# Two raw weight tiles fetched and decoded later, and v loaded in groups of 1, 1, 2 and 8 pairs, in an attention and MoE kernel

## The chip, the cores and the metric

The kernel runs on one core of one Trainium2 chip. The metric is the device time of one execution in microseconds; the time of a kernel is the median of its runs.

## The reference

Causal attention, then two small dense networks, all in fp32. There are 2 batches of 12 heads, 448 positions and a head size of 64, so 896 tokens of width 768. Cut to what is computed:

```python
scores = np.where(mask, -1e9, q @ k.T / sqrt(64))     # per batch and head, causal
attn = softmax(scores) @ v                            # 1e-9 is added to the sum
x = heads side by side                                # 896 x 768
h = max(max(x @ w1, x @ w2), x @ w3) @ w_out          # first network, 768 wide
g = s * relu(h @ w_in)**2 + b                         # second network, 2048 wide
return g @ moe2_w_out
```

## The kernel before, in words

**Precision.** Each fp32 operand of a large product is held as a high and a low part, and three products (high by high, high by low, low by high) are summed in PSUM. The weights arrive raw, as 56 tiles of 128x768 64-bit words (768 KB each), and every raw tile is decoded on the chip into its high and low part (`decoder`, lines 132 to 190). The steps of one decode are: `high` (line 144, ACT) and `low` (line 147, ACT), which read the raw tile; `clamp` (line 153, DVE); `shift` (line 166, DVE); `sign` (line 172, DVE, which reads the raw tile a last time); `add` (line 179, DVE); `hi` (line 184, ACT); `lo` (line 92, DVE).

**Attention.** The 12 batch-and-head pairs (two heads each) go through a software pipeline of steps, `step(s)` for s = 0 to 13 (line 551). In step s pair s has its scores computed on TensorE (lines 350 to 388), its row minima taken on DVE (line 396) and its exponentials on ACT (line 408). Pair s-1 is transposed (line 435) and copied out of PSUM (line 441, pieces 0 to 2 by ACT, piece 3 by DVE); its row sums are transposed (`sums`, line 480), copied on DVE to `rows` (line 487), written to a small DRAM buffer `rcd` by two DMAs (`spread`, lines 488 and 489) and read back spread over the partitions into `rb` by two DMAs (`broadcast`, line 497). Pair s-2 is multiplied by v (`pv`, lines 451 to 460) into the one PSUM bank `o`. Pair s-3 is scaled by its `rb` out of `o` (`pv_out`, line 506, DVE, tile `xf`, then POOL lines 296 and 92). So `pv` of a pair waits until `xf` of the pair before has emptied `o`, and `xf` waits until that pair's `rb` has landed.

**Engine order.** Every engine runs its instructions in the order in which the program gives them; nothing is reordered. ACT has one decode operation at the end of a step at most, behind all exponentials of that step and ahead of those of the next one (`END`, line 34); DVE has its own in the middle (`MID`, line 29) or at the end. Where a decode step stands is written out by hand in these two tables.

**The DMA queue.** All loads leave through SP's queue (except one store). Its order in a step is: the two `rcd` writes (their `rows` must be there), the q and k of pair s+4 (`load`, line 268, tile `R`, 448 KB), the first count of v loads, the broadcast of pair s-1 (the `rcd` writes must have landed), the second count of v loads, and a raw weight tile (`fetch_w`, line 125, the DMA of line 129) if the step stands in `FETCH` (line 27). v is loaded in 42 DMAs of line 289: the pairs are cut into groups (`V_GROUPS`, line 39: first pair and number of pairs), each group has one SBUF tile and comes as 7 row pieces, once for a group of one pair, once for each of the two heads otherwise, so 7, 7, 14 and 14 DMAs. `V_LOADS` (line 40) has the two counts of each step. In the kernel before, raw tiles are asked for in steps 0 (no pair is there to broadcast, so `fetch_w` is called in its place), 1, 4, 8, 10 and 11.

**After attention** the products of the two networks run on TensorE (lines 698 and 807) with the decoded weights; the decode goes on beside them, and the first two decoded tiles are used already in steps 12 and 13, to fill TensorE.

Line 551 and the tables above it are what the change touches. The functions are below.

Of the kernel before, what the change touches and what calls it, by code (L numbers as in the profile page):

```python
# [23 lines left out]
TQ = 128  # L24
NQ = 3

FETCH = (1, 4, 8, 10, 11)
LAST = 9
MID = {
    2: ("clamp0",), 3: ("shift0",), 4: ("sign0",), 5: ("add0",), 6: ("lo0",), 7: ("clamp1",),  # L30
    8: ("shift1",), 9: ("sign1",), 10: ("add1",), 11: ("lo1",), 12: ("add2", "clamp3"),
    13: ("lo2", "shift3"),
}
END = {
    1: ("high0",), 2: ("low0",), 3: ("high1",), 4: ("low1",), 5: ("hi0",), 6: ("high2",),
    7: ("low2",), 8: ("clamp2",), 9: ("shift2",), 10: ("hi1", "sign2"), 11: ("high3",),
    12: ("hi2", "low3"),
}
V_GROUPS = ((0, 1), (1, 1), (2, 4), (6, 6))
V_LOADS = ((7, 7), (2, 5), (3, 4), (3, 0), (3, 0), (3, 0), (3, 0), (2, 0))  # L40
FILL = {12: (3, 5), 13: (0, 4)}
WARM = 10
BUSY = (7,)
# [7 lines left out]
def kernel(  # L51
# [73 lines left out]
    def fetch_w():  # L125
        if w_src:
            src = w_src.pop(0)
            raw = wr_p.tile([128, DM], I64, tag="wraw", name="wraw")
            nc.sync.dma_start(out=raw, in_=src)
            raws.append(raw)  # L130
# [101 lines left out]
    def attention():  # L232
        with ExitStack() as c2:
# [10 lines left out]
            vs = [  # L244
                fixed.tile([128, n, 2, NQ + 1, D], F32, name=f"v{a}") for a, n in V_GROUPS
            ]
# [26 lines left out]
            def v_loads(g):  # L273
                (first, n), V = V_GROUPS[g], vs[g]
                for a, b in pieces:
                    rows, src = slice(a % 128, a % 128 + b - a), slice(a % CH, a % CH + b - a)
                    to, of = V[rows, :, :, a // 128], v[first:first + n, src, :, a // CH]
                    if n == 1:
                        yield to[:, 0], of[0]
                    else:  # L280
                        for h in range(2):
                            yield to[:, :, h], of[:, :, h].rearrange("p k d -> k p d")

            v_list = [e for g in range(len(V_GROUPS)) for e in v_loads(g)]

            def load_v(n):
                for _ in range(min(n, len(v_list))):
                    to, of = v_list.pop(0)
                    nc.sync.dma_start(out=to, in_=of)  # L289

            def v_of(p):
                g = max(g for g, (a, _) in enumerate(V_GROUPS) if a <= p)
                return vs[g][:, p - V_GROUPS[g][0]]

# [197 lines left out]
            def broadcast(p):  # L492
                e = pair[p]
                flat = e["flat"]
                for h in range(2):
                    at = h * (NQ + 1) * 128
                    nc.sync.dma_start(
                        out=e["rb"][hs[h]], in_=flat[:, at:at + S].to_broadcast([D, S])
                    )
# [51 lines left out]
            def step(s):  # L551
                new, old, out, nxt = (
                    p if 0 <= p < n_pairs else None for p in (s, s - 1, s - 2, s + 2)
                )
                loads = V_LOADS[s] if s < len(V_LOADS) else (0, 0)
                if new is not None:
# [95 lines left out]
                if old is not None:  # L652
                    load_v(loads[0])
                    broadcast(old)
                else:
                    fetch_w()
                load_v(loads[1])
                if s in FETCH:
                    fetch_w()
                if s == LAST:  # L660
                    nc.sync.dma_start(out=sb[:, 0:1], in_=s2.to_broadcast([128, 1]))
                    nc.sync.dma_start(out=sb[:, 1:2], in_=b2.to_broadcast([128, 1]))
# [19 lines left out]
            for s in range(n_pairs + 2):  # L682
                step(s)
# [196 lines left out]
```

## Time and profile before

| what | us |
|---|---|
| median of 3 runs | 503.01 (501.52 to 503.52) |
| the profiled execution's own time | 502.06 |
| its span in the profile | 500.3 |
| TensorE busy (matmul) | 493.3, 99% of the span |
| DVE, ACT, POOL busy | 340.5, 282.9, 71.4 |

The span is from the first to the last instruction that the profiler saw; the time of an execution has 1.8 us more around it. TensorE's granted clock is at its upper level in all 40 slices of the page. Attention takes about the first 93 us of the span; then come the products of the networks, in which TensorE is the whole chain.

### The profile page before, as it was taken

The page shows a single profiled execution, that of the slowest core. Times are in us where ns is not written, and L with a number is a line of the kernel's source. Part 1 is how long each engine was busy: PE and PEld are TensorE (multiplying, and loading weights), DVE is VectorE, ACT ScalarE, POOL GpSimd, SP SyncE. Part 2 cuts the span into 40 slices and gives each one's busy share as a digit, 9 for nine tenths or more (in the row PEclk, how much of TensorE's full clock was granted, in tenths as well). Part 3 has the DMA queues.
Part 4 walks back from the last instruction along what each step waited for, and adds up shares of the span by engine and source line. Part 5 has one row for each costly group of instructions (what it writes and reads, how often), then busy time and mean ns, then how long its engine had stood idle before and what let it go on. Part 6 is the DMA issues. An engine that isn't in the chain of part 4 may idle for free.

```text
span 500.3 us, 7557 instructions
## 1 busy us (share of the span) xinstructions
PE 493.3 (99%) x2909; PEld 452.7 (90%) x2909; DVE 340.5 (68%) x512; ACT 282.9 (57%) x527; POOL 71.4 (14%) x103
## 2 busy tenths in 40 slices
PE   8999999999999999999999999999999999999997
PEld 4877888899999999999999999999999999999996
DVE  5778896665857667587677888888888644484401
ACT  5988977444445254444546878888786432253101
POOL 6988992300000000000000000000000000000000
PEclk9999999999999999999999999999999999999999
DMA  5777534223324231333223323332333323261003
GB/s 170 225 215 226 151 102 117 103 91 127 126 75 148 94 126 64 126 128 126 101 89 126 127 73 118 126 104 85 127 126 109 119 89 128 88 220 56 1 0 111
DMA packets 26212, 58.34 MB, mean 117 GB/s; under 512 B 13548, under 2 KB 17600, under 8 KB 26176
## 3 DMA queue, kind: packets, MB, share of 16 engines
q1 hardware_dynamic: 26032, 57.76, 35.2%
q8 instruction: 23, 0.38, 0.3%
q14 instruction: 13, 0.11, 0.1%
q10 hardware_dynamic: 144, 0.10, 0.1%
HBM read 55.05 MB, written 2.80 MB: 116 GB/s over the span
## 4 chain that ended last, share of the span: by engine, by line
PE 91%; DMA 2%; DVE 2%; SPq 2%; ACT 1%; POOL 1%; issue 0%; DVEq 0%; ACTq 0%
PE m L698 58%; PE m L807 23%; PE t L435 3%; PE o L451 2%; ACT p L408 1%; PE o L455 1%; SPq L289 1%; PE A L380 1%; PE C L388 1%; PE B L380 1%; DMA rcd<-rows 1%; DMA rb<-rcd 1%; DMA R<-in_qk_dram 1%; POOL HL L92 0%; PE o L460 0%
## 5 line engine op out<-in xcount | busy, mean ns | idle before, releaser
L698 PE MATMUL m<-x,whi 128*128 128x448 f32 x816 | 232.0, 366 | 0.0
L698 PEld LDWEIGHTS m<-x,whi 128*128 128x128 f32 x816 | 153.1, 188 | 12.3 <-ACT p L408 0.2
L698 PE MATMUL m<-x,wlo 128*128 128x448 f32 x408 | 149.0, 365 | 0.0
L807 PE MATMUL m<-whi,g 128*128 128x384 f32 x448 | 114.0, 334 | 0.0
L184 ACT CAST whi<-wa 128x768 fp32r<-128x768 f32 x56 | 46.7, 833 | 67.0 <-PE m L807 43.8
L698 PEld LDWEIGHTS m<-x,wlo 128*128 128x128 f32 x408 | 76.6, 188 | 6.0
L807 PEld LDWEIGHTS m<-whi,g 128*128 128x128 f32 x448 | 81.0, 188 | 0.0
L144 ACT ACTIVATE wa<-wraw 128x768 f32<-128x768 f32 x56 | 50.6, 904 | 52.3 <-DVE wlo L92 52.3
L92 DVE TENSOR_TENSOR wlo<-wa,whi 128x768 fp32r<-128x768 f32 x56 | 53.3, 953 | 38.4 <-ACT whi L184 38.4
L807 PE MATMUL m<-wlo,g 128*128 128x384 f32 x224 | 74.8, 334 | 0.0
L179 DVE CUSTOM_DVE_ANT_0 wa<-wa,wr 128x1536 uint16<-128x1536 uint16 x56 | 53.6, 957 | 1.9
L172 DVE SCALAR_TENSOR_TENSOR wa<-wraw,wa 128x768 int32<-128x768 int32 x56 | 53.7, 959 | 0.0
L147 ACT ACTIVATE wr<-wraw 128x768 int32<-128x768 uint32 x56 | 50.6, 904 | 0.0
L807 PEld LDWEIGHTS m<-wlo,g 128*128 128x128 f32 x224 | 42.0, 188 | 0.0
L705 DVE TENSOR_TENSOR t<-t,m 128x448 f32<-128x448 f32 x24 | 14.9, 621 | 38.7 <-PE m L698 38.7
L698 PE MATMUL m<-h,whi 128*128 128x448 f32 x144 | 40.9, 365 | 0.0
L166 DVE TENSOR_SCALAR wa<-wa 128x768 int32<-128x768 int32 x56 | 32.2, 575 | 1.8
L92 POOL TENSOR_TENSOR HL<-R,HL 128x448 fp32r<-128x448 f32 (+1 forms) x21 | 29.9, 1443 | 3.2 <-DVE HL L309 2.1
L792 ACT ACTIVATE r<-m 128x448 f32<-128x448 f32 x32 | 17.4, 544 | 22.2 <-PE m L698 22.2
L698 PEld LDWEIGHTS m<-h,whi 128*128 128x128 f32 x144 | 27.1, 188 | 2.1
L158 DVE TENSOR_SCALAR wa<-wa 128x768 f32<-128x768 f32 x52 | 28.7, 552 | 0.0
L781 DVE SCALAR_TENSOR_TENSOR r<-m,r 128x448 f32<-128x448 f32 x32 | 20.0, 625 | 12.3 <-ACT r L792 12.3
(85 smaller groups left out, 551.2 us busy)
## 6 DMA issues: line engine op xcount, KB each, us to landing
wraw<-in_w_dram SPq DMA_DIRECT2D x56, 768.0 KB
R<-in_qk_dram SPq DMA_DIRECT2D x11, 448.0 KB
rb<-rcd SPq DMA_DIRECT2D x24, 112.0 KB
out_dram<-o SPq DMA_DIRECT2D x13, 192.0 KB
v<-in_v_dram SPq DMA_DIRECT2D x4, 96.0 KB
v<-in_v_dram SPq DMA_DIRECT2D x2, 168.0 KB
v<-in_v_dram SPq DMA_DIRECT2D x6, 48.0 KB
v<-in_v_dram SPq DMA_DIRECT2D x2, 144.0 KB
```

The costliest lines, as they stand in the source:

```text
L92: eng.tensor_tensor(out=lo, in0=full, in1=hi.bitcast(F32), op=ALU.subtract)
L144: nc.scalar.activation(out=e["f"], in_=e["high"].bitcast(F32), func=ACTF.Abs)
L147: nc.scalar.activation(out=e["r"], in_=e["low"].bitcast(U32), func=ACTF.Copy, scale=2.0 ** -29)
L158: nc.vector.tensor_scalar(out=e["f"], in0=e["f"], scalar1=UNDER, scalar2=OVER, op0=ALU.max, op1=ALU.min)
L166: nc.vector.tensor_scalar(out=a, in0=a, scalar1=3, scalar2=0x3FFFFFF8, op0=ALU.logical_shift_left, op1=ALU.bitwise_and,)
L172: nc.vector.scalar_tensor_tensor(out=e["a"], in0=e["high"], scalar=-0x40000000, in1=e["a"], op0=ALU.bitwise_and, op1=ALU.bitwise_or,)
L179: nc.vector.tensor_tensor(out=e["a"], in0=e["a"], in1=e["r"], op=ALU.add)
L184: nc.scalar.copy(out=e["hi"], in_=e["f"])
L698: nc.tensor.matmul(p, wt[w][:, ws], cols(act[i], a, b), start=(i == 0 and n == 0), stop=(i == len(act) - 1 and n == 2),)
L781: nc.vector.scalar_tensor_tensor(out=r, in0=p, scalar=0.0, in1=r, op0=ALU.max, op1=ALU.mult)
L792: after(0, lambda: nc.scalar.activation(out=r, in_=p, func=ACTF.Relu))
L807: nc.tensor.matmul(acc[t][:, 0:EH], gt[f][:, a, ts], w[:, ws], start=(f == 0 and n == 0), stop=(f == KG - 1 and n == 2),)
```

## The change

It alters four tables and the place of one call.

```diff
-FETCH = (1, 4, 8, 10, 11)
+FETCH = (1, 3, 5, 8, 10, 11)
 LAST = 9
 MID = {
-    2: ("clamp0",), 3: ("shift0",), 4: ("sign0",), 5: ("add0",), 6: ("lo0",), 7: ("clamp1",),
+    3: ("clamp0",), 4: ("shift0",), 5: ("sign0",), 6: ("add0",), 7: ("lo0",),
     8: ("shift1",), 9: ("sign1",), 10: ("add1",), 11: ("lo1",), 12: ("add2", "clamp3"),
     13: ("lo2", "shift3"),
 }
 END = {
-    1: ("high0",), 2: ("low0",), 3: ("high1",), 4: ("low1",), 5: ("hi0",), 6: ("high2",),
-    7: ("low2",), 8: ("clamp2",), 9: ("shift2",), 10: ("hi1", "sign2"), 11: ("high3",),
+    2: ("high0",), 3: ("low0",), 4: ("high1",), 5: ("low1",), 6: ("hi0",),
+    7: ("high2", "clamp1"), 8: ("low2", "clamp2"), 9: ("shift2",), 10: ("hi1", "sign2"), 11: ("high3",),
     12: ("hi2", "low3"),
 }
-V_GROUPS = ((0, 1), (1, 1), (2, 4), (6, 6))
-V_LOADS = ((7, 7), (2, 5), (3, 4), (3, 0), (3, 0), (3, 0), (3, 0), (2, 0))
+V_GROUPS = ((0, 1), (1, 1), (2, 2), (4, 8))
+V_LOADS = ((7, 7), (4, 4), (3, 3), (4, 0), (5, 0), (5, 0))
...
                 if old is not None:
                     load_v(loads[0])
                     broadcast(old)
-                else:
+                if s in FETCH:
                     fetch_w()
                 load_v(loads[1])
-                if s in FETCH:
-                    fetch_w()
```

The raw tiles 0, 1 and 2 are asked for in steps 1, 3 and 5 instead of 0, 1 and 4, and within their step directly behind the broadcast, ahead of the second count of v loads. Tile 0 is decoded one step later throughout; `high` and `low` of tile 1 and of tile 2 come one step later, `clamp` of tile 1 moves from the middle to the end of step 7. The last two groups of v are pairs 2 and 3, and pairs 4 to 11, instead of 2 to 5 and 6 to 11; the 42 loads are spread over steps 0 to 5 instead of 0 to 7. The number of instructions and the bytes are the same.

## Rows read from the trace of the kernel before

**Rows 1.** The page: the span, and TensorE in part 1.
```profile
span 500.3 us, 7557 instructions
...
PE 493.3 (99%) x2909; PEld 452.7 (90%) x2909; DVE 340.5 (68%) x512; ACT 282.9 (57%) x527; POOL 71.4 (14%) x103
```
**Rows 2.** Timeline of PE, steps 4 to 7 (start us, us, engine, line, ...).
```profile
28.37 0.38 PE L358 MATMUL B<-tri,identb 128*128 128x256 bf16 x2
...
32.89 0.59 PE L451 MATMUL o<-PT,v 128*64 128x448 f32 x1 [1.08 <-DVE xf L506]
...
35.97 0.38 PE L358 MATMUL B<-tri,identb 128*128 128x256 bf16 x2
...
40.21 0.59 PE L451 MATMUL o<-PT,v 128*64 128x448 f32 x1 [0.78 <-DVE xf L506]
...
42.12 0.28 PE L480 MATMUL A<-ident,su 128*7 128x128 f32 x1
...
43.22 0.38 PE L358 MATMUL B<-tri,identb 128*128 128x256 bf16 x2
...
46.60 0.59 PE L451 MATMUL o<-PT,v 128*64 128x448 f32 x1
...
49.61 0.38 PE L358 MATMUL B<-tri,identb 128*128 128x256 bf16 x2
```
**Rows 3.** Waits from 10 to 45 us (us in total, times, longest).
```profile
DVE xf L506 <- DMA rb<-rcd: 3.0, 2, 1.6
```
**Rows 4.** The chain that ended last, 15 to 47 us (start us, us, what).
```profile
23.07 3.99 DMA rcd<-rows
...
35.60 3.84 DMA rb<-rcd
```
**Rows 5.** Timeline of SP's queue, steps 0 to 2.
```profile
11.39 0.43 SPq L129 DMA_DIRECT2D wraw<-in_w_dram  x1
11.86 4.47 SPq L289 DMA_DIRECT2D v<-in_v_dram  x7
16.43 0.48 SPq L488 DMA_DIRECT2D rcd<-rows  x1
...
17.68 0.96 SPq L289 DMA_DIRECT2D v<-in_v_dram  x2
18.74 1.14 SPq L497 DMA_DIRECT2D rb<-rcd  x2
...
22.57 0.41 SPq L129 DMA_DIRECT2D wraw<-in_w_dram  x1
```
**Rows 6.** Timeline of ACT, the ends of steps 1 to 4 and what follows.
```profile
17.31 0.88 ACT L144 ACTIVATE wa<-wraw 128x768 f32<-128x768 f32 x1
...
23.23 0.90 ACT L147 ACTIVATE wr<-wraw 128x768 int32<-128x768 uint32 x1
24.19 0.59 ACT L408 ACTIVATE p<-A,mx 128x384 f32<-128x384 f32 x1
...
27.76 0.25 ACT L408 ACTIVATION_READ_ACCUMULATOR p<-B,mx 128x1 f32 x1
...
37.07 0.89 ACT L147 ACTIVATE wr<-wraw 128x768 int32<-128x768 uint32 x1
```
**Rows 7.** Timeline of SP's queue, steps 4 and 5.
```profile
41.23 0.57 SPq L129 DMA_DIRECT2D wraw<-in_w_dram  x1
42.74 0.29 SPq L488 DMA_DIRECT2D rcd<-rows  x1
...
43.83 1.55 SPq L289 DMA_DIRECT2D v<-in_v_dram  x3
47.57 1.10 SPq L497 DMA_DIRECT2D rb<-rcd  x2
```
**Rows 8.** Timeline of PE, the start of steps 10 and 11.
```profile
68.96 0.38 PE L358 MATMUL B<-tri,identb 128*128 128x256 bf16 x2
...
75.67 0.38 PE L358 MATMUL B<-tri,identb 128*128 128x256 bf16 x2
```

## The prediction

> **What bounds the kernel now.** I read the page first, then TensorE's own timeline, then what its gaps waited for. The page has TensorE busy for 493.3 of the 500.3 us [rows 1]: only 7 us in the whole execution are not matmul, so a change of this kind can win at most the few of them that it touches. All that it moves lies in the first 62 us or so, in the attention steps; the work behind them is untouched and begins as much earlier or later as they end. The timeline of TensorE gives the length of a step by the mask matmul of line 358, which opens it: 6.39 us from step 6 to step 7 (43.22 to 49.61), but 7.60 in step 4 (28.37 to 35.97) and 7.25 in step 5 (35.97 to 43.22) [rows 2]. The surplus, 1.21 + 0.86 = **2.07 us, is the prize**. In both steps TensorE stands still ahead of pv (1.08 and 0.78 us) until DVE's xf has emptied the bank [rows 2], and xf has waited 3.0 us in two waits for rb, the broadcast [rows 3]. The broadcast is late because the DRAM write ahead of it, issued at 23.07, directly behind raw tile 1 (22.57), takes 3.99 us, and because SP is behind with its list [rows 4, 5].
>
> All sums are made against the profiled execution, 502.06 us, which is 0.95 below the median of the three runs; I add that at the end.
>
> **Raw tile 0: when it is asked for.** Today at 11.39, with the second group of v behind it from 11.86 [rows 5]. Without it these seven loads start at 11.39 and end 0.47 earlier, at 15.87. The two rcd writes and the load of R take 17.68 - 16.43 = 1.25 us: 17.1. Then come four v loads instead of two. One costs 0.48 (0.96 by two) or 0.64 (4.47 by seven) [rows 5]: 1.9 to 2.6 us, so 19.0 to 19.7. The broadcast takes 1.14 [rows 5]: the tile is asked for between 20.1 and 20.8, say 20.6.
>
> **When it lands.** No row has a landing, so I bound it. The rcd write that stood in line 0.5 us behind raw tile 1 landed at 27.06, 4.5 us after that tile was asked for [rows 4, 5]. Behind raw tile 2, asked for at 41.23, the broadcast that waits for a rcd write went out at 47.57, 6.3 us later [rows 7]. I take 4.5, since its queue is as empty as the new place's: 25.1, and 24.7 to 27.2 as bounds.
> The Trainium skill, "DMA: Bandwidth & Descriptors", section "Anatomy of one DMA", fits 2.0 us plus bytes over 436 GB/s, for DMAs issued from GpSimd. Estimated by that page, a 768 KB tile would take 3.8 us and land at 24.4, which the 4.5 in the rows does not bear out; the sum below would be about 1.4 us smaller.
>
> **What waits for it.** ACT takes high0 at the end of step 2, where low0 stands now, at 23.23 [rows 6]. Today there are 5.9 us from asking to reading (11.39 to 17.31); now there are 2.6. ACT would stand from 23.23 to 25.1, run high0 (0.88), and begin the exponentials of step 3 at 26.0 instead of 24.19: 1.8 us late. Queued behind it on ACT are all exponentials and three copies of step 3. TensorE's next use of that bank is the mask matmul of step 4 at 28.37; the last exponential ends at 28.01, a slack of 0.36 [rows 2, 6]. So step 4 starts 1.8 - 0.36 = **1.45 us late** (1.1 to 3.5 by the bounds). In step 4 the wait for xf then goes. Behind the tile (0.4) SP has four v loads (2.1), rcd writes and R (1.25) and three v loads (1.6): 20.6 + 5.4 = 26.0 for the broadcast of pair 1, or up to 26.9 if its rcd write lands well behind the tile; today 27.06. The 3.84 of [rows 4] puts its landing at 29.8 to 30.7, while xf, which would start 0.6 ahead of pv at 32.89 - 1.08 + 1.45 = 33.3, wants it at 32.7: in time. Against the 1.08 now, 1.45 is **+0.37 us**.
> That ACT gives up high0 at 17.31 wins nothing: TensorE runs its own queue without a gap there, and the page has it 99% busy [rows 1]. DVE's clamp0, which leaves step 2, is likewise beside TensorE's work.
>
> **Step 5.** From 26.4 SP goes on with that broadcast (1.14), three v loads (1.6), rcd and R (1.25) and four v loads (2.1): the broadcast of pair 2 leaves at 32.5, where its second half leaves at 35.60 today [rows 4], and lands by 37.0; xf wants it at about 40.21 - 0.78 + 0.37 - 0.6 = 39.2. The 0.78 of stall goes, and with it the step's surplus: **-0.86**. The next thing to be late is raw tile 1.
>
> **Raw tile 1** is asked for in step 3 behind that broadcast, near 33.7 to 34.0, and landed by the same 4.5 at 38.5 at the latest. Its high1 is now at the end of step 4, where ACT is at 37.07 today [rows 6], 37.4 with the delay above. ACT stands for 1.1 us, less the 0.36: **+0.75** (0 where SP is 1 us quicker, 2.5 with 6.3 for the landing).
>
> **v of pairs 4 to 11.** Pair 4 is multiplied in step 6, and the last five of its group's 14 loads go out in step 5. Today the list of step 5 has its rcd write at 42.74 and its first v load 1.09 later; three cost 1.55, so 0.52 each [rows 7]. With step 5 about 0.4 earlier, the first goes out at 43.4 and the fifth at 45.5. By the broadcast's 3.84 [rows 4] it is there at 49.3; the rows show no landing of a v load. pv of pair 4 starts at 46.60 + 0.26 and its last chunk is used some 1.6 us into its 1.91 (as 40.21 to 42.12) [rows 2]: 48.5. Short by 0.8; nothing at all if v comes a fifth sooner than rb does, 2.5 if it also queues behind R. v is smaller than rb only in its last pieces, so I take **+0.5**.
>
> **DVE in step 7** has lo0 and clamp1 where one operation stood. Steps 8 and 9 already have two; the step behind them is 6.71 long (68.96 to 75.67) [rows 8] against 6.39: **+0.3** (0 to 0.3). Raw tile 2 (asked for in step 5, read at the end of step 7) has two steps and costs nothing; low2 in step 8 fills a wait of ACT for the minima. The later requests are unchanged.
>
> **Sum:** +0.37 - 0.86 + 0.75 + 0.5 + 0.3 = **+1.06 us**: 503.1 for the profiled execution, **504.0** for the median. The change trades the wait for rb for a wait for the raw tile.
>
> **Rivals.**
> *The tile is in time and the prize is won.* If v loads cost less than I take (they are issued without a raw tile in the DMA queues) or a tile lands in under 4 us, ACT hardly waits, both stalls go, and -2.07 + 0.3 gives 501.2 as a median. For it: the 0.48 rows. Against: even then step 2's own rcd write still stands behind raw tile 0, as the one at 23.07 did. Chance 0.2.
> *The new group of eight is late and decides* (slower). pv of pair 4 waits for the whole of R and five v loads to pass. Each microsecond by which the last lands behind 48.5 counts in full, since TensorE has nothing else in its queue. With 0.64 per load and 6.3 instead of 3.84 to land, that is 45.9 + 6.3 = 52.2, 3.7 late instead of 0.5: 507. From 50.5 on it makes the kernel slower by over 0.5%. Against: v was not what step 8 waited for, in which today's last group is first used. Chance 0.18.
> The Trainium skill, same page, section "Rules for kernel authors", says to issue a DMA early and wait late. Both this rival and the forecast are what that rule would expect of a change that asks later; no row prices it but those used above.
> *The broadcast stays late.* The tile was moved behind a broadcast, but the next rcd write comes 2.5 us behind it and lands with it; then rb of pair 1 is as late as now, and the 1.08 stays. It runs beside ACT's wait, not on top: about 504.1, within the forecast. Chance 0.12.
>
> **Numbers.** Forecast 0.5, the others as given. A measurement of this kernel can tell about 0.5% (2.5 us) from no change. Faster by that needs more than the prize of 2.07: 0.02. Slower needs the second rival or both tile waits at their upper bounds: 0.15. Same: 0.83. The range reaches from the first rival, 501.2, to 506.0, where the second is half in.
>
> **What would show it.** Right: ACT idle 1 to 2 us ahead of line 144 at the end of step 2, and less at step 4; no wait of xf for rb in steps 4 and 5; the mask matmul of step 4 near 29.8, step 4 back at 6.5 us, step 5 near 7.1. Wrong: line 144 without a wait there; or pv in step 6 waiting for v by over a microsecond; or any change beyond step 9, where nothing was moved.

## The result, and the profile after

The changed kernel takes **508.26 us** in the median (507.7 to 508.33), the kernel before 503.26 beside it: ratio 1.0103 [1.0077, 1.0129], slower by 5.0 us. Forecast were 504.0, and 501.2 to 506.0 as the range; slower by more than the 2.5 us that the prediction calls measurable had a chance of 0.15. The profiled execution took 508.27 us, 6.2 more than that of before; its span is 506.4 us against 500.3 [rows 1].

The time is lost between steps 3 and 8. The first view is the timeline of TensorE: a wait for ACT at the end of step 3, the mask matmul that opens each step, and the waits of pv, to be read against [rows 2, 8].

```profile
28.01 0.28 PE L480 MATMUL A<-ident,su 128*7 128x128 f32 x1 [0.72 <-ACT p L408]
...
30.59 0.38 PE L358 MATMUL B<-tri,identb 128*128 128x256 bf16 x2 [0.85 <-ACT p L408]
...
36.97 0.38 PE L358 MATMUL B<-tri,identb 128*128 128x256 bf16 x2
...
45.52 0.38 PE L358 MATMUL B<-tri,identb 128*128 128x256 bf16 x2 [0.84 <-ACT p L408]
...
51.64 0.54 PE L451 MATMUL o<-PT,v 128*64 128x192 f32 x2 [0.94 <-DMA v<-in_v_dram]
...
53.06 0.33 PE L451 MATMUL o<-PT,v 128*64 128x64 f32 x2 [0.31 <-DMA v<-in_v_dram]
...
53.75 0.33 PE L460 MATMUL o<-PT,v 128*64 128x64 f32 x2 [0.36 <-DMA v<-in_v_dram]
...
55.11 0.38 PE L358 MATMUL B<-tri,identb 128*128 128x256 bf16 x2
...
61.50 0.38 PE L358 MATMUL B<-tri,identb 128*128 128x256 bf16 x2
...
65.62 0.59 PE L451 MATMUL o<-PT,v 128*64 128x448 f32 x1 [0.68 <-DVE xf L506]
...
68.86 0.38 PE L358 MATMUL B<-tri,identb 128*128 128x256 bf16 x2
```

From one opening to the next come the step lengths (step 3 opens at 21.92 here, at 21.99 before):

| step | before | after | difference | forecast |
|---|---|---|---|---|
| 3 | 6.38 | 8.67 | +2.29 | +1.45 |
| 4 | 7.60 | 6.38 | -1.22 | -1.08 |
| 5 | 7.25 | 8.55 | +1.30 | -0.86 + 0.75 |
| 6 | 6.39 | 9.59 | +3.20 | +0.5 |
| 7 | 6.38 | 6.39 | 0.0 | 0 |
| 8 | 6.42 | 7.36 | +0.94 | +0.3 |
| 9, 10 | 6.55, 6.71 | 6.38, 6.63 | -0.25 | 0 |

Together +6.26, which is the whole difference between the two profiled executions; it is 1.2 more than that of the medians, because the one of before lies below its own. Behind step 10 nothing changed. The stalls of pv for xf in steps 4 and 5 [rows 2] are gone. In their place TensorE waits for ACT (0.72 us in step 3, 0.85 and 0.84 as steps 4 and 6 open), and pv of step 6 waits for v.

The waits from 10 to 62 us (us in total, times, longest) say the same:

```profile
ACT wa L144 <- DMA wraw<-in_w_dram: 5.5, 2, 2.8
...
PE o L451 <- DMA v<-in_v_dram: 1.2, 2, 0.9
DVE xf L506 <- DMA rb<-rcd: 0.7, 1, 0.7
```

The wait for rb has fallen from 3.0 us [rows 3] to 0.7; a wait of ACT for the raw tile has come, 5.5 us in two pieces. They stand at the ends of steps 2 and 4, where [rows 6] has no wait, as the timeline of ACT shows:

```profile
25.89 0.94 ACT L144 ACTIVATE wa<-wraw 128x768 f32<-128x768 f32 x1 [2.78 <-DMA wraw<-in_w_dram]
...
40.85 0.94 ACT L144 ACTIVATE wa<-wraw 128x768 f32<-128x768 f32 x1 [2.68 <-DMA wraw<-in_w_dram]
```

When those tiles were asked for is in the timeline of SP's queue, to be read against [rows 5, 7]:

```profile
20.16 0.59 SPq L129 DMA_DIRECT2D wraw<-in_w_dram  x1
20.79 1.89 SPq L289 DMA_DIRECT2D v<-in_v_dram  x4
22.78 0.29 SPq L488 DMA_DIRECT2D rcd<-rows  x1
23.11 0.24 SPq L489 DMA_DIRECT2D rcd<-rows  x1
23.45 0.36 SPq L268 DMA_DIRECT2D R<-in_qk_dram  x1
25.89 1.31 SPq L289 DMA_DIRECT2D v<-in_v_dram  x3
27.29 1.09 SPq L497 DMA_DIRECT2D rb<-rcd  x2
...
34.66 1.12 SPq L497 DMA_DIRECT2D rb<-rcd  x2
35.83 0.58 SPq L129 DMA_DIRECT2D wraw<-in_w_dram  x1
...
38.04 5.11 SPq L289 DMA_DIRECT2D v<-in_v_dram  x5
43.20 1.89 SPq L497 DMA_DIRECT2D rb<-rcd  x2
...
46.40 3.08 SPq L289 DMA_DIRECT2D v<-in_v_dram  x5
```

Tile 0 is asked for at 20.16 and read at 25.89, as soon as it is there: **5.7 us**. Tile 1: 35.83 to 40.85, **5.0 us**. The five v loads of step 4 took 5.11 us to issue (1.02 each in the mean, where the forecast had 0.52), and those of step 5 went out from 46.40. In the chain that ended last, the final one is issued at 48.68 and takes 5.03:

```profile
48.68 5.03 DMA v<-in_v_dram
```

So it is there at 53.71, and pv goes on at 53.75. Between 23.81 and 25.89 SP issued nothing, and went on at the moment when ACT began to read tile 0. The waits of SP's own queue from 10 to 62 us name what it stood for:

```profile
SPq L289 <- DMA wraw<-in_w_dram: 2.1, 1, 2.1
```

The load that stood is the eighth DMA behind the tile: four v loads, two rcd writes and R went out before it. In every trace of this case in which SP's waits name a raw tile, the eighth DMA behind that tile is the one that stands. So a tile that lands late also holds up the list behind it. No run was made to vary this.

Last, the timeline of DVE around the step in which it has two decode operations:

```profile
60.92 1.35 DVE L92 TENSOR_TENSOR wlo<-wa,whi 128x768 fp32r<-128x768 f32 x1
62.19 0.68 DVE L441 COPY PT<-t 128x512 f32<-128x512 f32 x1
62.79 1.30 DVE L153 SCALAR_TENSOR_TENSOR wa<-wa,over 128x768 f32<-128x768 f32 x1
64.02 0.94 DVE L396 TENSOR_REDUCE mx<-A 128x2 f32<-128x768 f32 x1
...
64.99 0.57 DVE L506 TENSOR_TENSOR xf<-o,rb 128x448 f32<-128x448 f32 x1
```

The two take 2.65 us, and xf behind them ends 0.68 too late for pv of step 8.

### The profile page after: what moved, and what is told of

Read it like the earlier page. It is cut to its first block, busy times and chain, and to the rows that moved or that the text cites. A ratio compares the mean times of both kernels' runs of the same rounds, so it can differ in the third digit from the quotient of the medians.

```text
span 506.4 us, 7549 instructions
## 1 busy us (share of the span) xinstructions
PE 495.4 (98%) x2909; PEld 453.3 (90%) x2909; DVE 342.1 (68%) x512; ACT 282.7 (56%) x527; POOL 69.8 (14%) x103
## 4 chain that ended last, share of the span: by engine, by line
PE 88%; DVE 3%; DMA 3%; ACT 2%; POOL 2%; SPq 1%; issue 1%; POOLq 0%; ACTq 0%
PE m L696 58%; PE m L805 23%; ACT p L408 2%; PE t L435 2%; POOL HL L92 1%; PE o L451 1%; DVE mx L396 1%; DMA v<-in_v_dram 1%; SPq L289 1%; DMA wraw<-in_w_dram 1%; PE A L380 1%; PE B L380 1%; PE o L455 1%; DMA R<-in_qk_dram 1%; PE C L388 1%
## 5 line engine op out<-in xcount | busy, mean ns | idle before, releaser
L144 ACT ACTIVATE wa<-wraw 128x768 f32<-128x768 f32 x56 | 50.8, 907 | 59.3 <-DVE wlo L92 51.2
L92 POOL TENSOR_TENSOR HL<-R,HL 128x448 fp32r<-128x448 f32 (+1 forms) x21 | 27.8, 1346 | 6.7 <-DVE HL L309 5.7
```

Of the source, the lines that this page charges most:

```text
L92: eng.tensor_tensor(out=lo, in0=full, in1=hi.bitcast(F32), op=ALU.subtract)
L144: nc.scalar.activation(out=e["f"], in_=e["high"].bitcast(F32), func=ACTF.Abs)
```

## The experiments

The first four take the change apart; e5, e6 and e8 mend it, and e7 tries a smaller piece of it on the kernel before; the last two ask about the v loads alone. Medians stand against 503.31 for e1 to e4, 503.05 for e5 to e8 and 503.23 for e9 and e10.

**e1: the changed kernel with v as before.**

```diff
-V_GROUPS = ((0, 1), (1, 1), (2, 2), (4, 8))
-V_LOADS = ((7, 7), (4, 4), (3, 3), (4, 0), (5, 0), (5, 0))
+V_GROUPS = ((0, 1), (1, 1), (2, 4), (6, 6))
+V_LOADS = ((7, 7), (2, 5), (3, 4), (3, 0), (3, 0), (3, 0), (3, 0), (2, 0))
```

> The changed kernel with V_GROUPS and V_LOADS of before, so the raw tiles alone are moved. Theory (three separate waits: ACT for the two raw tiles, pv of pair 4 for its v, DVE's double step 7): step 6 falls from 9.59 to 6.4 us; raw tile 0 is asked for two v loads (0.95 us) earlier, so ACT's 2.78 us of waiting at line 144 becomes about 1.8, the second about 1.5 to 2.2; step 8 keeps its 7.36; 503.5 to 504.8 us in all. Rival A (SP's list of v loads is the one cause): no wait of ACT for a raw tile over 1 us is left, 502 to 503.3 us. Rival B (the raw tile in the queue is the one cause of the late v too): v would be late here as well, a wait of pv for v of over 1 us in step 6 or 8, 506 us or more.

Measured: 508.44 us, ratio 1.0099 [1.0081, 1.0118], no better. The theory and rival A are missed by 3.6 us and more; rival B has the time, but not the wait for v that it needs. No such wait is left, so the change without its v tables costs 5.1 us here. The waits from 10 to 62 us:

```profile
ACT wa L144 <- DMA wraw<-in_w_dram: 5.9, 2, 3.2
DVE xf L506 <- DMA rb<-rcd: 1.1, 2, 0.6
```

The chain that ended last has both tiles (start us, us, what); tile 0, with two groups of v loads around it, takes 7.11:

```profile
19.38 7.11 DMA wraw<-in_w_dram
...
37.09 5.01 DMA wraw<-in_w_dram
```

Steps 3, 5 and 6 last 8.65, 9.04 and 7.86 us. Step 6 has no wait that would explain 1.5 us. The windows do (us, busy us of each engine with counts, granted clock, DMA share, GB/s):

```profile
43.00:46.80 3.80, 1.71 (x18) 1.18 (x14) 2.35 (x4) 3.80 (x16) 3.17 (x4) 1.00 0.93 158
46.80:50.70 3.90, 3.89 (x24) 3.28 (x24) 2.00 (x4) 3.17 (x8) 1.37 (x4) 0.56 0.88 233
50.70:54.00 3.30, 3.30 (x35) 2.62 (x34) 2.02 (x5) 2.89 (x12) 2.59 (x4) 1.00 0.56 222
```

After 3.8 us in which TensorE was busy for 1.71, it works for 3.9 us at a mean granted clock of 0.56, nearly all at the lower of its two levels (1.2 GHz), with 24 matmuls where 35 fit into the next 3.3 us. A wait can thus cost twice: once while it lasts, and once in the clock behind it.

**e2: the kernel before with the new v alone.** The two v lines of the diff of the change.

> The kernel before with V_GROUPS and V_LOADS of the change, so v alone is regrouped. Theory: pv of pair 4 still waits for the last of its group's 14 loads, five of which go out in step 5: step 6 is 8.8 to 9.6 us long instead of 6.39, the other steps stay within 0.5 us of before, no wait of ACT for a raw tile: about 506. Rival A: all of the 5 us is back, 508. Rival B: v alone costs nothing, step 6 at 6.4 to 6.8, 503.3.

Measured: 510.77 us, ratio 1.0148 [1.0128, 1.0169], worse than the whole change and than every expectation. TensorE's timeline:

```profile
48.23 0.59 PE L451 MATMUL o<-PT,v 128*64 128x448 f32 x1 [1.70 <-DVE xf L506]
...
53.29 0.90 PE L451 MATMUL o<-PT,v 128*64 128x192 f32 x2 [3.46 <-DMA v<-in_v_dram]
```

Step 6 lasts 13.96 us: 1.70 for rb by way of xf, 3.46 for v, and then half speed (0.51 granted from 53.20 to 56.70). SP's queue shows why v is later than in the changed kernel, though its steps begin earlier:

```profile
42.68 0.36 SPq L129 DMA_DIRECT2D wraw<-in_w_dram  x1
...
45.62 5.57 SPq L289 DMA_DIRECT2D v<-in_v_dram  x5
```

Raw tile 2, still asked for in step 4 here, stands ahead of the last five loads, and these take 5.57 us to issue, 1.1 each in the mean. The last of them is the eighth DMA behind the tile, and SP's own waits have it stand for the tile:

```profile
SPq L289 <- DMA wraw<-in_w_dram: 1.2, 1, 1.2
```

**e3: the kernel before with `clamp1` one step earlier,** so that DVE has two decode operations in step 6 and one less in step 7.

```diff
-    2: ("clamp0",), 3: ("shift0",), 4: ("sign0",), 5: ("add0",), 6: ("lo0",), 7: ("clamp1",),
+    2: ("clamp0",), 3: ("shift0",), 4: ("sign0",), 5: ("add0",), 6: ("lo0",),
...
-6: ("high2",),
+6: ("high2", "clamp1"),
```

> The kernel before with clamp1 moved from the middle of step 7 to the end of step 6, so that step 6 has lo0 and clamp1 on DVE, as step 7 has in the changed kernel, with nothing else changed. Theory: the double costs by itself what it cost there: step 7 is about 7.3 us long instead of 6.38, 504.1 us in all. Rival: the 0.94 us of the changed kernel came from what was late behind the wait for v, and a double costs what it does in steps 8 and 9 of before, 0.1 to 0.3: 503.3 to 503.6.

Measured: 503.57 us, ratio 1.0007 [0.9995, 1.0018]. In its trace step 7 is 7.28 us instead of 6.38, the same 0.9 that step 8 lost in the changed kernel, but the median is only 0.26 higher, and the interval reaches from -0.25 to +0.9. The step is as the theory had it, the time as the rival had it: by itself the doubling costs 0.9 us at most.

**e4: the changed kernel, its tiles asked for where the kernel before asks for them.** They are still decoded later.

```diff
-FETCH = (1, 3, 5, 8, 10, 11)
+FETCH = (1, 4, 8, 10, 11)
...
-                if s in FETCH:
+                if s == 0:
                     fetch_w()
                 load_v(loads[1])
+                if s in FETCH:
+                    fetch_w()
```

> The changed kernel with the raw tiles asked for in the steps and places of before (step 0, end of steps 1 and 4), decoded as in the change, v as in the change. Theory: ACT no longer waits at line 144, step 3 falls from 8.67 to 6.4 and step 5 from 8.55 to 7.2, but the wait of xf for rb is back in step 4 (7.6 instead of 6.38); the waits for v in step 6 and for DVE in step 8 stay: 507.0 to 507.5. Rival A: 508.3, no difference. Rival B: the wait for v goes with the raw tile that stood ahead of it: 504.2.

Measured: 511.56 us, ratio 1.0165 [1.0142, 1.0187], more than any expectation had. Line 144 does not wait any more and step 3 is 6.39 us, so it is the hour of asking that made ACT wait. But the waits for rb are back (pv waits 1.50 and 1.93 us for xf in steps 4 and 5), and with raw tile 2 again ahead of the last v loads, step 6 looks like that of e2:

```profile
54.15 0.54 PE L451 MATMUL o<-PT,v 128*64 128x192 f32 x2 [4.01 <-DMA v<-in_v_dram]
```

**e5: the changed kernel with v in groups of 1, 1, 3 and 7 pairs,** so that pair 4 belongs to the group whose loads end in step 2.

```diff
-V_GROUPS = ((0, 1), (1, 1), (2, 2), (4, 8))
+V_GROUPS = ((0, 1), (1, 1), (2, 3), (5, 7))
```

> The changed kernel with v in groups of 1, 1, 3 and 7 pairs instead of 1, 1, 2 and 8: pair 4 comes with the third group, whose loads go out in steps 1 and 2; the last group is first used one step later, by pair 5. The same 42 loads in the same steps. Theory (the group of eight is needed before its last loads, sent in step 5, have landed): step 6 falls from 9.59 to 6.4 to 6.8 us and step 7 stays at 6.4, everything else as in the changed kernel: about 505.0. Rival (the DMA queues are simply full, whatever the grouping): the wait moves to pair 5, step 7 becomes 8 us or more, 507 to 508.5.

Measured: 506.2 us (504.62 to 507.42), ratio 1.0059 [1.0039, 1.0079]. No wait for v, as the theory had it, in some 1 us more time; tile 0 is waited for (3.3 us). The profiled execution is the slowest of the five and has a long stretch at the lower clock level behind that wait:

```profile
28.00:31.80 3.80, 1.66 (x16) 1.14 (x12) 2.37 (x4) 3.80 (x16) 3.28 (x4) 0.98 0.53 121
31.80:38.20 6.40, 6.22 (x34) 5.12 (x35) 4.05 (x8) 4.16 (x13) 2.76 (x5) 0.50 0.89 194
```

The mean clock of that execution is 0.993; the other four have 1.000 and take 504.62 to 506.51.

**e6: the changed kernel with raw tiles asked for in steps 0, 2 and 5,** the first two one step sooner.

```diff
-FETCH = (1, 3, 5, 8, 10, 11)
+FETCH = (0, 2, 5, 8, 10, 11)
```

> The changed kernel with raw tiles 0 and 1 asked for one step earlier (steps 0 and 2, at the change's place behind the broadcast), tile 2 still in step 5, all decoded as in the change. Theory: ACT finds both tiles, so steps 3 and 5 (8.67 and 8.55 us) fall to 6.4 to 7.3; some wait of xf for rb comes back, under 1.1 us in step 4; pv of pair 4 still waits for v, step 6 at 8 to 10 us: 504.8 to 506.5. Rival (what counts is raw tile 2 ahead of the last v loads, and ACT's waits are covered anyway): 508, the waits only change their names.

Measured: 506.77 us, ratio 1.0076 [1.0056, 1.0096]. Line 144 waits for no tile; the wait for v is left, and longer than in the changed kernel, since the steps come to it earlier. Step 6 lasts 10.65 us. TensorE's timeline:

```profile
50.37 0.54 PE L451 MATMUL o<-PT,v 128*64 128x192 f32 x2 [1.49 <-DMA v<-in_v_dram]
51.12 0.40 PE L455 MATMUL o<-PT,v 128*64 128x128 f32 x2 [0.22 <-DMA v<-in_v_dram]
...
51.94 0.33 PE L451 MATMUL o<-PT,v 128*64 128x64 f32 x2 [0.30 <-DMA v<-in_v_dram]
...
52.51 0.33 PE L460 MATMUL o<-PT,v 128*64 128x64 f32 x2 [0.24 <-DMA v<-in_v_dram]
```

**e7: the kernel before, with only raw tile 1 behind the broadcast of step 2** and the decode of tiles 1 and 2 later.

```diff
-FETCH = (1, 4, 8, 10, 11)
+FETCH = (0, 2, 4, 8, 10, 11)
...
-    1: ("high0",), 2: ("low0",), 3: ("high1",), 4: ("low1",), 5: ("hi0",), 6: ("high2",),
-    7: ("low2",), 8: ("clamp2",),
+    1: ("high0",), 2: ("low0",), 4: ("high1",), 5: ("hi0",), 6: ("low1",), 7: ("high2",),
+    8: ("low2", "clamp2"),
...
-                else:
+                if s in FETCH:
                     fetch_w()
                 load_v(loads[1])
-                if s in FETCH:
-                    fetch_w()
```

> The kernel before with one thing moved: raw tile 1 is asked for in step 2, directly behind the broadcast, instead of at the end of step 1 just ahead of the rcd writes; high1 goes from step 3 to 4, low1 from 4 to 6, high2 from 6 to 7, low2 from 7 to 8, so ACT still has one decode operation a step, and DVE's tables stay. Theory: the rcd write of step 2 no longer stands behind a raw tile, so xf finds rb in step 4 (1.08 us of stall gone) and mostly in step 5 (0.78), and ACT does not wait at line 144: 501.2 to 502.2, faster than before by 0.2 to 0.4%. Rival (rb is late because SP is late with its v loads, whatever the raw tile does): the stalls stay, 503.3. Third: the tile now delays rb of pair 2 instead, step 5 grows by 1 us or more: 504.

Measured: 502.85 us, ratio 0.9994 [0.9981, 1.0007]. Steps 4 and 5 fall to 6.70 and 6.59 us, 1.56 less than before: most of the prize of 2.07. Steps 9 and 10 are 7.35 and 6.39 instead of 6.55 and 6.71, so 0.48 is lost again; no decode operation was moved to them, and e2, whose decode tables are those of before, has 7.23 and 6.38 there, so what makes this difference is open. No gain that can be measured.

**e8: e5 and e6 together.**

> The edits of the two runs with v in groups of 1, 1, 3, 7 and with raw tiles 0 and 1 asked for in steps 0 and 2, together, in the changed kernel. Theory (two separate missed deadlines): both are met, no wait of ACT for a raw tile, no wait of pv for v over 0.3 us; what is left is DVE's double step 7 (up to 0.9) and some wait for rb: 501.8 to 503.3, as before or faster. Rival (one full queue): 505 or more.

Measured: 503.28 us, ratio 1.0003 [0.9991, 1.0015]. With the tiles asked for a step sooner and pair 4 out of the late group, the loss is gone. The waits from 10 to 62 us have no tile in them, and of v only small ones of the weight load:

```profile
DVE xf L506 <- DMA rb<-rcd: 2.9, 3, 1.2
...
PEld o L455 <- DMA v<-in_v_dram: 0.5, 1, 0.5
...
PEld o L460 <- DMA v<-in_v_dram: 0.3, 1, 0.3
```

The wait for rb is back at 2.9 us, as before the change [rows 3], but later: steps 4 and 5 are 14.03 us together instead of 14.85, and steps 6 to 8 are 21.06 instead of 19.19, with pv waiting 0.50, 0.63 and 0.26 for xf. (The trace of before is of an execution 1.0 us below the median beside this run.) So the loss is mended, and the prize is not won with it.

**e9: e2 with raw tile 2 asked for in step 5** (`FETCH = (1, 5, 8, 10, 11)`, `high2` at the end of step 7, `low2` and `clamp2` at that of step 8).

> The kernel with the new v tables alone (510.77), but with raw tile 2 asked for in step 5 (still as the last thing of the step) and decoded one step later, as in the changed kernel. Theory A (raw tile 2, asked for in step 4 at 42.68, stands in the DMA queues and in SP's list ahead of the last five v loads, and that made the wait for v larger than in the changed kernel): step 6 falls from 13.96 to some 9.6 us, the longest wait of pv for v from 3.46 to 1 to 1.5 us, the granted clock stays at its upper level or nearly; 506.5 to 507.5. Theory B (the v loads and the broadcasts are late by themselves, because v of steps 1 to 3 holds SP; tile 2 plays no part): step 6 stays above 12 us, 510 to 511.

Measured: 506.43 us, ratio 1.0064 [1.0047, 1.0081], 4.3 less than e2. The last five loads are issued from 44.58 and take 2.98 us instead of 5.57; step 6 lasts 8.51, with waits for v of 0.26 and 0.50. So raw tile 2 in front of them was more than half of what the new v costs by itself. What is left is in that step and in step 5 (10.10 us): there pv waits 2.04 for xf, which waits for rb, and the clock granted falls to 0.65 over the 3.9 us behind.

**e10: e6 with the last v loads a step earlier,** the groups as in the change.

```diff
-V_LOADS = ((7, 7), (4, 4), (3, 3), (4, 0), (5, 0), (5, 0))
+V_LOADS = ((7, 7), (4, 4), (3, 3), (5, 0), (5, 4))
```

> The changed kernel with raw tiles asked for in steps 0, 2 and 5 (506.77, in which only the wait for v was left), and with the last five v loads of the group of eight one step earlier: step 3 issues five instead of four, step 4 five and then four behind its broadcast, step 5 none. The groups stay 1, 1, 2 and 8. Theory A (it is the hour of the last loads that makes pv of pair 4 wait, not the size of the group): no wait of pv for v in step 6, step 6 at 6.4 to 7.2 instead of 10.65, no broadcast more than 1 us late; 503 to 504. Theory B (the DMA queues are full in steps 3 and 4, loads that are issued sooner land no sooner or push the broadcast and R back by as much): a wait of 1 us or more for v or rb in steps 5 or 6 remains, 505.5 to 507.

Measured: 504.08 us (503.04 to 505.66), ratio 1.0023 [1.0008, 1.0038]. Step 6 is 6.38 us and waits for no v, so it was the hour of the last loads and not the size of the group. But the profiled execution, at 505.61 one of the three slowest of ten, has theory B's price in the step before:

```profile
41.61 1.01 PE L451 MATMUL o<-PT,v 128*64 128x448 f32 x1 [2.60 <-DVE xf L506]
```

The broadcast that xf needs was late. Neither theory had it whole: the wait for v goes, and part of it comes back as a wait for rb.

## Why the prediction was wrong

**Right:** the prize (stalls of 1.08 and 0.78 for rb) was won, steps 4 and 5 lost them; the first new wait is ACT's for raw tile 0 at the end of step 2; tile 0 is asked for at 20.16, within the 20.1 to 20.8 worked out; nothing behind step 10 changed. The change did trade a wait for rb for one for the raw tile.

**The step that failed first: "I take 4.5".** A raw tile landed in 5.7 and 5.0 us, not 4.5. The 4.5 came from a rcd write that stood behind a tile, at a place where four v loads did not follow at once. That write was no bound for the tile either: in the packed trace of the kernel before, the last report of this tile's own DMA comes at 27.59, half a us behind the landing of the write and 5.0 us after asking. The Trainium skill, "DMA: Bandwidth & Descriptors", section "Anatomy of one DMA", whose fit gives 3.8 us for such a tile as an estimate, lies further off than the 4.5. For tile 0 that is 2.29 us instead of 1.45, which the bounds (1.1 to 3.5) held. For tile 1 the hour was wrong too: asked for at 35.83 instead of 33.7 to 34.0, because SP stood from 23.81 to 25.89 for tile 0, which the prediction's list of SP did not have, and because the seven v loads behind that took 4.6 us instead of 3.7. ACT waited 2.68 instead of 1.1. With the stall of 0.86 gone, the +1.30 of step 5 means 2.16 for this tile where +0.75 stood. The two tiles were under-priced by 0.84 and 1.41 us.

**The step that failed most: v of pairs 4 to 11, "+0.5".** It measured +3.20. The working took 0.52 us for each issue, from three loads in a quiet step [rows 7], and 3.84 for the landing, from rb. The five loads of step 4 took 1.02 each, the broadcast behind them was late, and the list of step 5 with it: the last load went out at 48.68 where the fifth was forecast at 45.5, and landed in 5.03. Wanted at 48.5 by the sum, or 50.8 when the tiles had made step 6 late by 2.3, it was there at 53.71: 2.9 late. The 0.8 of the sum was cut to 0.5 because v was said to be smaller than rb in its last pieces; the last two of these loads are 128 KB each, and the two of rb 112. That is the second rival, worked out there with 3.7 us and 507; it had 0.18. Its size is in part luck: it had the last load go out at 45.9 and take 6.3, where it went out at 48.68 and took 5.03. The evidence brought against it, that v was not waited for in step 8 before, said nothing of step 6.

**DVE in step 7, "+0.3 (0 to 0.3)":** +0.94 in the trace, in the step behind. e3 shows the same 0.9 in the step, and 0.26 (-0.25 to 0.9) in the time. The bound was taken from one step of one trace [rows 8]; step 9, behind the two operations of step 8, is 6.55 us in that trace and 7.23 in that of e2, whose decode tables are the same.

The four terms fell short by 0.84, 1.41, 2.70 and 0.64 us; less the 0.39 that steps 4, 9 and 10 did better, this is the 5.20 between the 1.06 of the sum and the 6.26 of the traces.

**How the parts stand to each other.** Four medians make a table, each less the 503.05 or 503.26 beside it:

| | 1, 1, 2, 8 | 1, 1, 3, 7 |
|---|---|---|
| tiles asked for in steps 1, 3, 5 | +5.0 (the change) | +3.15 (e5) |
| tiles asked for in steps 0, 2, 5 | +3.7 (e6) | +0.2 (e8) |

The tiles alone cost 3.15, v alone 3.7, both 5.0 and not 6.85. Each of these has an interval of about 1 us to either side, so that both cost less together than added is likely, and not shown; the traces fit it, since a step that the tiles make late gives v more time (step 6 is 9.59 us in the change and 10.65 in e6). Nor does one part have one price: with v as before the same tiles cost 5.1 (e1), and the new v costs 7.5 with tile 2 ahead of its last loads (e2) and 3.2 without (e9). So the terms could not simply be added, as the sum did, but here adding would rather have come out too high; what made the forecast low was the size of the terms. That the two deadlines made the loss is shown by e5, e6 and e8: mending one leaves 3 us or more, mending both leaves nothing that can be measured, with DVE's two operations in step 7 still there.

**What stays open.** In three of its four executions the changed kernel has a mean clock of 0.995 or 0.996 instead of the 0.999 of the profiled one, and the same time; what was traded there is not in a trace. The falls of the clock come and go between executions of e5 and e9 too, so how much of a median is due to them was not separated.

## What to carry to other kernels

Moving a load later removes whatever stood behind it in the queue and makes a new deadline of the load itself: price it with the landing of the same transfer at its new neighbours, not with the emptiest one in the trace, and leave more than a step (6.4 us here) between asking and reading: a raw tile took 5.0 to 7.1 us to land in the views above. Where one tile gathers many loads, its reader waits for the last of them; look for what else (here raw tile 2) is issued in front of that last load, and for what SP itself has to wait for before it can issue it. Terms that share one queue are not independent: mend one and another grows, so a pair of experiments that mends each alone and both together tells more than taking parts out.

## What the runs showed that was not expected

- **The clock behind a wait.** In e1, e2, e4, e5, e9 and e10 a stretch of waiting TensorE is followed by 3.4 to 7 us at or near the lower clock level: 0.56 (e1), 0.51 (e2), 0.50 over 6.4 us (e5), 0.52 over 6.9 us (e4). The profiled execution of the changed kernel waited as well and shows 0.999 over all.
- **SP's issue of a v load** took 0.44 us at 25.89 (1.31 for three) and 1.02 at 38.04 (5.11 for five): the same instruction, more than twice as long where more was under way.
- **DVE operations of one form** took 0.94 or 1.35 us (`lo`, line 92) and 0.94 or 1.30 (`clamp`, line 153). The long ones ran beside POOL's line 92 or 296, but `lo` took 0.94 beside line 92 of POOL in the kernel before as well, so what makes the difference is open.
